# Scores of an attention's first batch in half rows of the TensorE array

## The chip, the cores and the metric

One Trainium2 chip (trn2), of which the kernel uses one core. The metric is the device time of one execution, in microseconds (us); the median of three runs of the kernel before is 1106.93 us (1106.71 to 1107.18).

## What is computed

An attention over blocks of 64 positions, whose result is fed to a two-layer network with a leaky ReLU. All inputs are float32.

```python
B, H, S, D = 8, 8, 576, 64                      # q, k, v
scores = matmul(q, k.transpose) / sqrt(D)
scores = where(pos_i // 64 >= pos_j // 64, scores, -1e9)
attn = softmax(scores)                          # sum + 1e-9 below the line
x = (attn @ v) as (B * S, H * D)                # 4608 x 512
out = maximum(0.01 * h, h) @ w_out,  h = x @ w_in   # 512 x 2048, 2048 x 512
```

## The kernel before

The work is attention for 64 heads (8 batches of 8) and a network (here FFN) over 18 chunks of 256 tokens. FFN chunks run as soon as the eight heads of their tokens are done, between the matmuls of later heads. The FFN matmuls (lines 847 and 866) take each operand as a high and a low part in fp32r: three products of one pass each, w_in as wih and wil, w_out as woh and wol, x as xh and xl (made by split_x), g as gh and gl.

The order of the work is written by a planner, class Plan. Each piece of work has a rank (roughly the head it belongs to plus a due time), one or several engines with a cost in ns, and keys that it reads and writes; run() goes through time, gives each free engine its ready piece of lowest rank, and writes the instructions down in that order. The planner's costs decide the order and on which of VectorE (DVE), ScalarE (ACT) and GpSimd (POOL) a copy or a subtraction runs; nothing is decided on the chip. multiply() is its model of TensorE: 109 ns (LOAD) and a stream per matmul, RATE = 0.449 ns per column, doubled before 8 us (SLOW).

A head's scores are cut in five tiles of up to 128 queries; tile t has kw[t] = 64, 192, 320, 448, 576 keys. The first batch (heads 0 to 7) is done in two halves so that the FFN can begin early: eight pieces "lo" with tiles 0, 1 and 2, then eight pieces "hi" with tiles 3 and 4. For these 16 pieces plain_s holds: the scores are float32 matmuls straight from qk_in (line 488), without high and low parts. q and k lie twice in qk_in, in partitions 0 to 63 and again in 64 to 127, since the host repeats them; the matmul runs over all 128 rows, so it adds each product twice, and the copy at line 464 scales q by scale / 2. Each float32 matmul is two matmul records on TensorE. Line 489 is that matmul, and line 491 its cost for the planner, four times the rate:

```python
go = lambda ...: nc.tensor.matmul(
    ap, qkt()[:rows, 0, cols], qkt()[:rows, 1, k0:k1], start=first, stop=last
)
yield 4 * RATE * (k1 - k0), go
```

The scores go to PSUM, p_s of two banks (odd "lo" pieces use p_h). order_a tells where a tile lies: in "lo" tiles 2 and 1 share bank 0 and tile 0 has bank 1; in "hi" tile 3 lies in bank 0, and tile 4, made after it, is two matmuls of 288 columns, one in each bank. After a group of scores, DVE masks (line 513) and takes the maximum (520), ACT takes the exponent (529), DVE sums and inverts (544, 545), one of three engines scales (558 to 560), TensorE transposes (594), ACT or DVE copies (ptf), and TensorE multiplies with v (664, in the shape 128 rows by 64 columns) into x.

In the same first part of the kernel the weights are brought in as 32 pieces of float64 words that DVE, ACT and POOL turn into float32 and into high and low parts (weight_piece: val, wih, wil, woh, wol). Later batches make their scores at line 498 in fp32r.

Of the kernel before, what the change touches and what calls it, by code (L numbers as in the profile page):

```python
# [57 lines left out]


LOAD = 109  # L60
RATE = 0.449
SLOW = 8000


class Plan:
# [37 lines left out]
    def run(self):  # L103
# [7 lines left out]
        since = [0] * total  # L111
        waiting = []
        ready = {e: [] for e in ("PE", "DVE", "ACT", "POOL", "SP")}
        free = dict.fromkeys(ready, 0)
        port = {"DVE": 0, "POOL": 0}
        order, now, moved, done = [], 0, 0, 0
        start, stream = 0, 0

        def offer(i):
            for k, choice in enumerate(self.ops[i][0]):  # L120
# [11 lines left out]
                if not left[j]:  # L132
                    offer(j)

        def multiply(matmuls, at):
            nonlocal start, stream
            for cost, fn in matmuls:
                if now < SLOW:
                    cost *= 2
                start = max(start + stream, max(start, at) + LOAD, now)  # L140
                stream = cost
                order.append(fn)
            return start + stream
# [4 lines left out]
        while done < total:  # L148
# [6 lines left out]
            for e, q in ready.items():  # L155
# [5 lines left out]
                if other:  # L161
                    open_ = port[other] <= now
                    can = [x for x in q if not ends[x[1]] and (open_ or (e == "DVE" and self.ops[x[1]][0][x[2]][0] == "DVE"))]
                    if not can:
                        wake.append(port[other])
                        continue
                    x = min(can)
                    q.remove(x)
                    heapq.heapify(q)
                elif e == "PE":  # L170
                    x = heapq.heappop(q)
                    if self.ops[x[1]][4] == "long":
                        self.fill = None
                    free[e] = multiply(self.ops[x[1]][0][x[2]][1], since[x[1]])
                    end(x[1], e, free[e])
                    continue
                else:
                    x = heapq.heappop(q)
# [48 lines left out]
def attention_ffn(ctx: ExitStack, tc: tile.TileContext, qk: bass.AP, v: bass.AP, w_in: bass.AP, w_out: bass.AP, out: bass.AP):  # L227
# [191 lines left out]
    def attention(i):  # L419
# [17 lines left out]
        def row(t, n, c, w):  # L437
            at, c0 = {0: (3, 256), 1: (3, 0), 2: (4, 0)}[t] if odd else (t, 0)
            return prow[y][at][:n, c0 + c : c0 + c + w]

        def pkeys(t):
            if odd:
                return [("p", 0, {0: 5, 1: 3, 2: 4}[t])]
            return [("p", y if t else 0, t)] + ([("p", 0, 5)] if kind == "hi" and t == 3 else [])
# [16 lines left out]
        rp = r0 - RP  # L461
        q_in, k_in = lambda: qkt()[:rows, 0, qa:qe], lambda: qkt()[:rows, 1, :ke]
        if plain_s:
            add(copying(qe - qa, q_in, q_in, by=scale / 2), rp, [], [qkey])
            qkd = [qkey]
        else:
            qd, khd, kld = qs[z][:, qa:qe], kh[z][:, :ke], kl[z][:, :ke]
# [14 lines left out]
        def scores(tiles):  # L482
            banks = [bank for bank, _ in tiles]
            for y, (b, (t, ap, k0, k1, c)) in enumerate(tiles):
                first, last = b not in banks[:y], b not in banks[y + 1 :]
                cols = slice(q0[t], q0[t] + P)
                if plain_s:
                    go = lambda ap=ap, cols=cols, k0=k0, k1=k1, first=first, last=last: nc.tensor.matmul(  # L488
                        ap, qkt()[:rows, 0, cols], qkt()[:rows, 1, k0:k1], start=first, stop=last
                    )  # L490
                    yield 4 * RATE * (k1 - k0), go
                    continue
                if c == BOTH:
                    moving = ks[z][:, :, k0:k1]
# [9 lines left out]

        def softmax(tiles, mms, masks, r, both=None):
            banks = sorted({(sk, bk) for _, _, bk in tiles for bk in bk})
            add([("PE", list(scores(mms)))], r, qkd, banks)
            if both is not None:
                add([merging(*both, BLK)], r, [], banks)

# [52 lines left out]
        lay = order_a[kind]  # L563
        tiles = [(t, scored(k)[:, c : c + kw[t]], (k,)) for t, k, c in lay]
        at = {t: (bk[0], ap) for t, ap, bk in tiles}
        if plain_s:
            mms = [(bk[0], (t, ap, 0, kw[t], 0)) for t, ap, bk in tiles]
        else:
            mms = [(at[t][0], (t, at[t][1], 0, kw[t], c)) for t, c in turns[kind]]
        pair = lambda ap, step: ap.rearrange("p (a b) -> p a b", b=BLK)[:, 0 : step + 1 : step]  # L570
        masks = [ap[0:64, kw[t] - 64 : kw[t]] for t, ap, _ in tiles if t]
        if kind == "full":
            masks = [pair(p_s[:BLK].rearrange("p a b -> p (a b)")[:, 384:832], 6)]
        softmax(tiles, mms, masks, r0)
        if kind != "lo":
            tiles = [(4, p_s[:, :, 0:288], (0, 1))]
# [205 lines left out]
    def bank():  # L782
# [2 lines left out]

    order_a = {
        "full": ((3, 0, 0), (2, 1, 0)),
        "lo": ((2, 0, 0), (1, 0, 320), (0, 1, 0)),
        "hi": ((3, 0, 0),),
    }  # L790
    turns = {
# [164 lines left out]
```

## Time and profile before

| what | us |
|---|---|
| median of three runs (lowest, highest) | 1106.93 (1106.71, 1107.18) |
| span of the profiled execution, first to last instruction | 1104.7 |
| what the median has beyond that span | 2.2 |
| TensorE busy (share of the span) | 1075.9 (97%) |
| VectorE, ScalarE, GpSimd busy | 808.9, 685.0, 437.8 |
| matmul records | 6792 |

The profiled execution has no time of its own beside its span, so the median less the span stands for what lies around it. A matmul record begins where its stream begins and ends some time after the next has begun, so the price of one is taken from start to start and not from its duration. A write of a PSUM tile by line 488 is called a group here: the three matmuls of a "lo" piece, or those of tile 3 or of tile 4 of a "hi" piece; there are 24. FFN start is the first matmul of line 847.

### The profile page before, as it was taken

Reading aid. Unit: us, or ns where it says so; the run is one execution under the profiler, and the core shown is the slowest. Engines: PE = TensorE matmul, PEld = TensorE weight load, DVE = VectorE, ACT = ScalarE, POOL = GpSimd, SP = SyncE. Lnnn points to the kernel's source line nnn. Section 1 sums busy time; section 2 is a strip of 40 time slices with the busy share of each in tenths; the row PEclk is TensorE's granted clock in tenths of the full one; section 3 lists DMA queues with packets and bytes.
Section 4 is the critical chain, followed back from the end, with each engine's and each line's share of the span. In section 5 each row is a group of like instructions: output and inputs, shape, how many; then the busy total and the mean of one; then the engine's idle time right before and its main releaser. Section 6 shows DMA issues by size and latency. Waiting matters only on the chain.

```text
span 1104.7 us, 19959 instructions
## 1 busy us (share of the span) xinstructions
PE 1075.9 (97%) x6792; PEld 951.1 (86%) x6792; DVE 808.9 (73%) x2001; ACT 685.0 (62%) x1664; POOL 437.8 (40%) x371
## 2 busy tenths in 40 slices
PE   5799999999999999999999999999999999999998
PEld 4577887788888999988999999989999999999997
DVE  5999867689989998976666799898989998400000
ACT  6887776577866777654655667767676766322222
POOL 2332421035754455433523455545454444412221
PEclk9999999999999999999999999999999999999999
DMA  6766432157775766654464476667676655100000
GB/s 223 219 210 203 151 115 60 52 163 210 214 205 171 204 182 199 181 168 128 129 171 120 120 216 179 202 173 208 188 209 187 203 168 161 44 20 20 1 20 20
DMA packets 94245, 166.19 MB, mean 150 GB/s; under 512 B 9664, under 2 KB 79296, under 8 KB 94144
## 3 DMA queue, kind: packets, MB, share of 16 engines
q1 hardware_dynamic: 94144, 164.93, 50.9%
q8 instruction: 53, 0.87, 0.3%
q14 instruction: 48, 0.39, 0.1%
HBM read 111.41 MB, written 53.48 MB: 149 GB/s over the span
## 4 chain that ended last, share of the span: by engine, by line
PE 77%; DVE 11%; ACT 6%; DMA 2%; issue 2%; SPq 0%; POOL 0%; ACTq 0%; DVEq 0%; POOLq 0%
PE p_h L847 29%; PE p_o L866 29%; PE p_s L498 6%; PE p_t L682 5%; PE p_t L664 4%; ACT prow L529 2%; DVE turn L745 2%; PE p_t L594 2%; DMA ptm<-way 2%; DVE nmrec L520 2%; PE p_s L488 2%; DVE qs L471 1%; ACT prow L560 1%; DVE pt L253 1%; ACT pt L243 1%
## 5 line engine op out<-in xcount | busy, mean ns | idle before, releaser
L847 PE MATMUL p_h<-xh,wih 128*128 128x256 f32 x1152 | 323.5, 281 | 1.7 <-ACT g L854 1.7
L847 PE MATMUL p_h<-xl,wih 128*128 128x256 f32 x1152 | 320.6, 278 | 0.7 <-DVE xl L253 0.6
L847 PE MATMUL p_h<-xh,wil 128*128 128x256 f32 x1152 | 319.9, 278 | 0.0
L254 POOL TENSOR_TENSOR gl<-g,gh 128x512 fp32r<-128x512 f32 x105 | 141.9, 1351 | 423.5 <-ACT gh L243 383.0
L847 PEld LDWEIGHTS p_h<-xh,wih 128*128 128x128 f32 x1152 | 216.5, 188 | 11.3 <-ACT g L854 2.1
L847 PEld LDWEIGHTS p_h<-xl,wih 128*128 128x128 f32 x1152 | 216.9, 188 | 10.6 <-DVE xl L253 1.3
L847 PEld LDWEIGHTS p_h<-xh,wil 128*128 128x128 f32 x1152 | 216.7, 188 | 0.0
L854 ACT ACTIVATE g<-p_h 128x512 f32<-128x512 f32 x144 | 85.8, 596 | 194.9 <-PE p_h L847 186.8
L529 ACT ACTIVATE prow<-p_s,nmrec 128x576 f32<-128x576 f32 (+4 forms) x308 | 160.0, 527 | 59.6 <-DVE nmrec L520 55.2
L866 PE MATMUL p_o<-woh,gh 128*128 128x512 f32 x576 | 181.2, 396 | 0.0
L866 PE MATMUL p_o<-woh,gl 128*128 128x512 f32 x576 | 179.3, 393 | 0.0
L866 PE MATMUL p_o<-wol,gh 128*128 128x512 f32 x576 | 179.0, 392 | 0.0
L254 POOL TENSOR_TENSOR pt<-ptm,pt 128x448 fp32r<-128x448 f32 x111 | 143.1, 1299 | 21.9 <-ACT pt L243 12.6
L745 DVE STREAM_TRANSPOSE turn<-prow 128x384 f32<-128x384 f32 (+3 forms) x384 | 141.2, 397 | 7.6 <-ACT prow L560 5.7
L520 DVE TENSOR_REDUCE nmrec<-p_s 128x1 f32<-128x576 f32 (+4 forms) x308 | 137.8, 480 | 2.6
L560 ACT ACTIVATE prow<-prow,nmrec 128x320 f32<-128x320 f32 (+4 forms) x231 | 110.9, 519 | 44.4 <-DVE nmrec L545 44.1
L866 PEld LDWEIGHTS p_o<-woh,gl 128*128 128x128 f32 x576 | 108.2, 188 | 24.1
L866 PEld LDWEIGHTS p_o<-wol,gh 128*128 128x128 f32 x576 | 108.2, 188 | 23.4
L498 PE MATMUL p_s<-ks,qs 128*128 128x288 f32 (+4 forms) x616 | 107.6, 307 | 3.9 <-ACT prow L529 3.6
L498 PEld LDWEIGHTS p_s<-ks,qs 128*128 128x128 f32 x616 | 89.2, 188 | 11.7 <-ACT prow L529 7.0
L866 PEld LDWEIGHTS p_o<-woh,gh 128*128 128x128 f32 x576 | 92.5, 188 | 5.9 <-issue 3.2
L243 ACT CAST pt<-ptm 128x448 fp32r<-128x448 f32 x182 | 90.7, 567 | 3.6 <-DMA ptm<-way 3.5
(83 smaller groups left out, 1422.5 us busy)
## 6 DMA issues: line engine op xcount, KB each, us to landing
way<-turn SPq DMA_DIRECT2D x192, 224.0 KB, 2.4
ptm<-way SPq DMA_DIRECT2D x192, 224.0 KB, 4.3
qk_in<-in_qk SPq DMA_DIRECT2D x56, 576.0 KB, 4.8
out<-ob SPq DMA_DIRECT2D x35, 256.0 KB, 2.4
raw<-in_w_in SPq DMA_DIRECT2D x16, 512.0 KB, 4.3
raw<-in_w_out SPq DMA_DIRECT2D x16, 512.0 KB, 4.3
v_stage<-in_v SPq DMA_DIRECT2D x48, 160.0 KB, 2.3
qk_in<-in_qk SPq DMA_DIRECT2D x8, 320.0 KB, 4.5
```

Of the source, the lines that this page charges most:

```text
L243: one = lambda: nc.scalar.copy(dst(), src())
L254: ("POOL", pool2(n), lambda: nc.gpsimd.tensor_sub(dst(), one(), two())),
L498: go = lambda ap=ap, cols=cols, moving=moving, first=first, last=last: nc.tensor.matmul(ap, qs[z][:, cols], moving, start=first, stop=last)
L520: [("DVE", dve(kw[t]), lambda t=t, ap=ap, flat=flat: nc.vector.tensor_reduce(nm[z][: qn[t], at_col[t] : at_col[t] + 1], ap[: qn[t]], axis= ...
L529: nc.scalar.activation(o, ap[: qn[t]], AF.Exp, bias=nm[z][: qn[t], at_col[t] : at_col[t] + 1], scale=1.0, accum_out=sums[z][: qn[t], at_co ...
L560: ("ACT", act(kw[t], True), lambda: nc.scalar.mul(p(), p(), by)),
L664: nc.tensor.matmul(to, vf[z][:, j], src, start=start, stop=stop)
L682: nc.tensor.matmul(to, vs[:, j, :], src, start=start, stop=stop)
L745: nc.vector.transpose(dst, src.rearrange("p (s b i) -> p s b i", b=4, i=32))
L847: nc.tensor.matmul(hh[:, i, :], w[:, d, f * P : (f + 1) * P], x[:, d, :], start=k == 0, stop=k == len(terms) - 1)
L854: add([("ACT", act(512), lambda: nc.scalar.activation(g, hh, AF.Prelu, alpha=0.01))], rank, [("h", z)], ["g"])
L866: nc.tensor.matmul(p_o[m], a[:, i, m * P : (m + 1) * P], w[:, 2 * u + i, :], start=u == 0 and k == 0, stop=u == NU - 1 and k == 5,)
```

## The change

The scores of the first batch use half of the array's rows for each matmul. Bank 0 of the two gets its scores from partitions 0 to 63 of qk_in, bank 1 from 64 to 127, so that a product is added once and q is scaled by scale. In "lo" tile 1 goes to bank 1 with tile 0 (320 columns in one bank, 256 in the other); in "hi" tile 3 is cut like tile 4, in two matmuls of 224 columns. The planner is told that such a matmul costs half of before, and that TensorE pays 100 ns (CHANGE) each time it goes from whole rows to half rows or back. Line numbers of the changed kernel are higher by 5 (scores) to 10 (transposes 604, values 674, FFN 857 and 876).

```diff
+CHANGE = 100
...
-        def multiply(matmuls, at):
-            nonlocal start, stream
+        def multiply(matmuls, at, half):
+            nonlocal start, stream, halved
+            if half != halved:
+                start, stream, halved = max(start + stream + CHANGE, now), 0, half
...
-            add(copying(qe - qa, q_in, q_in, by=scale / 2), rp, [], [qkey])
+            add(copying(qe - qa, q_in, q_in, by=scale), rp, [], [qkey])
...
-                    go = lambda ap=ap, cols=cols, k0=k0, k1=k1, first=first, last=last: nc.tensor.matmul(
-                        ap, qkt()[:rows, 0, cols], qkt()[:rows, 1, k0:k1], start=first, stop=last
+                    half = slice(64 * b, 64 * b + 64)
+                    go = lambda ap=ap, half=half, cols=cols, k0=k0, k1=k1, first=first, last=last: nc.tensor.matmul(
+                        ap, qkt()[half, 0, cols], qkt()[half, 1, k0:k1], start=first, stop=last
                     )
-                    yield 4 * RATE * (k1 - k0), go
+                    yield 2 * RATE * (k1 - k0), go
...
-            add([("PE", list(scores(mms)))], r, qkd, banks)
+            add([("PE", list(scores(mms)))], r, qkd, banks, kind="half" if plain_s else None)
...
-        if plain_s:
+        if kind == "hi":
+            tiles = [(3, p_s[:, :, 0:224], (0, 1))]
+            mms = [(k, (3, p_s[:, k, 0:224], 224 * k, 224 * k + 224, 0)) for k in range(2)]
+        elif plain_s:
...
-        "lo": ((2, 0, 0), (1, 0, 320), (0, 1, 0)),
+        "lo": ((2, 0, 0), (1, 1, 0), (0, 1, 192)),
```

The planner writes another order with these costs. On TensorE it differs from before up to row 870 of its list and is the same, row for row, behind it; DVE, ACT and POOL too differ only in the first quarter of their lists. Three places are shown (names as in the code; a number at a row's end counts equal rows in a row).

TensorE around the FFN start, before: L488 is a group of scores, L594 a transpose, L847 the FFN's first layer.

```order
107 L488 MATMUL p_s<-qk_in_124 128x448
108 L594 MATMUL p_t_99<-ident,prow_3_74 128x128
109 L594 MATMUL p_t_99<-ident,prow_4_75 128x128
110 L594 MATMUL p_t_99<-ident,prow_3_74 128x128
111 L594 MATMUL p_t_99<-ident,prow_4_75 128x128
112 L594 MATMUL p_t_98<-ident,prow_3_74 128x128
113 L594 MATMUL p_t_98<-ident,prow_4_75 128x128
114 L594 MATMUL p_t_98<-ident,prow_3_74 128x128
115 L594 MATMUL p_t_98<-ident,prow_4_75 128x128 x2
116 L488 MATMUL p_s<-qk_in_124 128x288 x2
117 L847 MATMUL p_h_100<-xh,wih 128x256
```

The same place of the changed kernel (L493 scores, L674 values, L857 FFN, L604 transposes).

```order
105 L674 MATMUL p_t_98<-ptf,vf_123 64x64
106 L493 MATMUL p_s<-qk_in_84 128x288 x2
107 L493 MATMUL p_s<-qk_in_124 128x224 x2
108 L857 MATMUL p_h_100<-xh,wih 128x256
109 L857 MATMUL p_h_100<-xl,wih 128x256
...
119 L857 MATMUL p_h_100<-xh,wil 128x256
120 L604 MATMUL p_t_99<-ident,prow_3_74 128x128
121 L604 MATMUL p_t_99<-ident,prow_4_75 128x128
```

The nine transposes of the first "hi" piece and the scores of the second one's tile 4 stood ahead of the FFN start, and now stand behind it; all that is ahead of it otherwise is the same work.

DVE of the changed kernel just ahead of that FFN start; before, the subtraction that makes xl was row 33 of POOL's list.

```order
106 L402 SCALAR_TENSOR_TENSOR val_119<-raw_116,val_119 128x512
107 L518 MEMSET p_s 64x64
108 L525 TENSOR_REDUCE nmrec<-p_s 128x1
109 L250 TENSOR_SCALAR val_120<-raw_117 128x512
110 L256 TENSOR_TENSOR xl<-xr_96,xh 128x1024
```

The subtraction moved from POOL to DVE, and the conversion to xh ahead of it from DVE to ACT.

## Rows read from the trace of the kernel before

**Rows 1.** The page's part 1, and the chain that ended last by engine (part 4).

```profile
PE 1075.9 (97%) x6792; PEld 951.1 (86%) x6792; DVE 808.9 (73%) x2001; ACT 685.0 (62%) x1664; POOL 437.8 (40%) x371
...
PE 77%; DVE 11%; ACT 6%; DMA 2%; issue 2%; SPq 0%; POOL 0%; ACTq 0%; DVEq 0%; POOLq 0%
```

**Rows 2.** Windows: length, busy us and records by engine, granted clock, DMA share, GB/s.

```profile
4.70:20.20 15.50, 12.06 (x52) 8.92 (x52) 10.13 (x33) 10.45 (x29) 3.94 (x5) 1.00 0.75 241
20.20:23.60 3.40, 0.03 (x1) 0.02 (x1) 3.27 (x11) 3.35 (x15) 0.59 (x1) 1.00 0.93 327
23.60:30.40 6.80, 6.75 (x23) 4.69 (x23) 5.05 (x15) 3.45 (x12) 0.67 (x1) 0.50 0.45 140
30.40:56.50 26.10, 19.43 (x108) 13.30 (x107) 23.56 (x66) 23.77 (x70) 9.88 (x8) 1.00 0.76 235
56.50:130.00 73.50, 73.04 (x445) 59.49 (x443) 68.77 (x149) 55.67 (x114) 21.55 (x15) 1.00 0.62 191
130.00:211.00 81.00, 81.00 (x506) 65.28 (x505) 54.84 (x145) 55.53 (x150) 16.79 (x19) 1.00 0.27 84
211.00:240.00 29.00, 29.00 (x173) 22.66 (x172) 21.59 (x62) 17.93 (x49) 4.34 (x4) 1.00 0.37 116
```

**Rows 3.** Timeline of all engines around the FFN start: start, length, instruction.

```profile
53.67 2.54 POOL L254 TENSOR_TENSOR xl<-xr,xh 128x1024 fp32r<-128x1024 f32 x1
56.50 0.50 PE L847 MATMUL p_h<-xh,wih 128*128 128x256 f32 x1
56.68 0.68 DVE L399 SCALAR_TENSOR_TENSOR val<-raw,val 128x512 int32<-128x512 int32 x1
```

**Rows 4.** TensorE's timeline, groups of scores and what follows them.

```profile
4.75 2.39 PE L488 MATMUL p_s<-qk_in 128*128 128x320 f32 x6 [4.75 <-ACT qk_in L246]
16.75 1.20 PE L488 MATMUL p_s<-qk_in 128*128 128x320 f32 x6
17.78 0.28 PE L594 MATMUL p_t<-ident,prow 128*128 128x128 f32 x1
25.49 2.23 PE L488 MATMUL p_s<-qk_in 128*128 128x320 f32 x6
27.66 2.18 PE L664 MATMUL p_t<-ptf,vf 128*64 128x64 f32 x8
113.23 1.15 PE L594 MATMUL p_t<-ident,prow 128*128 128x128 f32 x9
114.13 0.71 PE L866 MATMUL p_o<-woh,gh 128*128 128x512 f32 x2
```

**Rows 5.** TensorE's timeline inside one tile 4 group, windows that begin at each record.

```profile
123.19 0.40 PE L488 MATMUL p_s<-qk_in 128*128 128x288 f32 x1
123.43 0.65 PE L488 MATMUL p_s<-qk_in 128*128 128x288 f32 x2
123.67 0.65 PE L488 MATMUL p_s<-qk_in 128*128 128x288 f32 x2
```

**Rows 6.** TensorE's timeline at a step from whole shape to 128 by 64.

```profile
118.34 0.62 PE L866 MATMUL p_o<-woh,gh 128*128 128x512 f32 x2
118.80 0.62 PE L866 MATMUL p_o<-wol,gh 128*128 128x512 f32 x2
119.26 0.63 PE L866 MATMUL p_o<-woh,gl 128*128 128x512 f32 x2
119.81 0.43 PE L664 MATMUL p_t<-ptf,vf 128*64 128x256 f32 x1
```

**Rows 7.** DVE's groups by form, 0 to 130 us: count, busy us, mean ns, idle before.

```profile
L399 DVE SCALAR_TENSOR_TENSOR val<-raw,val 128x512 int32<-128x512 int32 x32 | 23.1, 723 | 0.1
L253 DVE TENSOR_TENSOR wol<-val,woh 128x512 fp32r<-128x512 f32 x12 | 9.3, 774 | 0.0
L244 DVE COPY ptf<-p_t 128x512 f32<-128x512 f32 x7 | 4.8, 682 | 1.1 <-PE p_t L594 1.0
```

**Rows 8.** Whom DVE waited for, 8 to 56 us: total, times, longest.

```profile
DVE p_h L513 <- PE p_h L488: 1.8, 2, 1.2
```

More of the change, by code (lines that the diff above doesn't have):

```diff
@@ L116, in run @@
         order, now, moved, done = [], 0, 0, 0
-        start, stream = 0, 0
+        start, stream, halved = 0, 0, False
         def offer(i):
@@ L173, in run @@
                         self.fill = None
-                    free[e] = multiply(self.ops[x[1]][0][x[2]][1], since[x[1]])
+                    free[e] = multiply(self.ops[x[1]][0][x[2]][1], since[x[1]], self.ops[x[1]][4] == "half")
                     end(x[1], e, free[e])
@@ L570, in attention @@
         pair = lambda ap, step: ap.rearrange("p (a b) -> p a b", b=BLK)[:, 0 : step + 1 : step]
-        masks = [ap[0:64, kw[t] - 64 : kw[t]] for t, ap, _ in tiles if t]
+        masks = [ap[0:64, kw[t] - 64 : kw[t]] for t, ap, _ in tiles if t and kind == "lo"]
         if kind == "full":
             masks = [pair(p_s[:BLK].rearrange("p a b -> p (a b)")[:, 384:832], 6)]
+        elif kind == "hi":
+            masks = [p_s[0:64, 1, 160:224]]
         softmax(tiles, mms, masks, r0)
```

## The prediction

> **What bounds the kernel now.** I read the page first: TensorE is busy for 1075.9 of 1104.7 us, and 77% of the chain that ended last is TensorE [rows 1]. So it matters where TensorE is *not* busy, and that is what the windows show [rows 2]. From the FFN start at 56.50 us [rows 3] to 240 us TensorE has 73.04 + 81.00 + 29.00 us of work in 183.5 us: a microsecond of TensorE work saved or added there moves all that follows, by as much. Ahead of 56.50 us TensorE is idle for 18.2 us (56.5 less 12.06 + 0.03 + 6.75 + 19.43), and what ends that stretch is something else: the first FFN matmul begins at 56.50, 0.29 us after POOL has ended xl (53.67 + 2.54 = 56.21) [rows 3], while VectorE is busy for 23.56 and ScalarE for 23.77 of the 26.10 us before [rows 2]. The order behind TensorE's row 870 is unchanged, which is at about 211 us in the trace, inside the full stretch. So the sum has two terms: when the FFN starts, and how much TensorE work lies behind that start. What comes later is moved along as it is.
>
> **What a group of scores costs.** A float32 matmul is two records. Inside a tile 4 group the records start at 123.19, 123.43 and 123.67 [rows 5]: 0.24 us for 288 columns, so four records take 0.97 us. By columns, tile 3 (two records of 448) takes 2 x 0.375 = 0.75 us. The three matmuls of a "lo" piece take 17.78 - 16.75 = 1.03 us, and about twice that where the engine ran at the lower of its two clocks: 27.66 - 25.49 = 2.17 us, in a stretch with a granted clock of 0.50 (1.2 GHz) [rows 2, 4].
>
> What the changed group costs no row shows, since no two matmuls of before sit in different halves of the rows. It lies between two ends. If nothing overlaps, tile 4 still has four records of 0.24 us, and tile 3 four of 0.19. If the halves run fully side by side, it is half. I take three quarters, by the order in which the records stand: bank 0's two records come first and both need rows 0 to 63, so the second waits for the first, as at 123.19 and 123.43; only then comes bank 1's first record, which can run beside it; bank 1's second is alone. That is three streams in place of four: 0.73 us for tile 4 and 0.56 for tile 3. A "lo" group goes from 576 to 416 columns, by 28%. The Trainium skill (TensorE: Matmul & The Clock Gate, Part 3: Packing small matmuls) has matmuls start and end strictly in program order and overlap when they sit in different row groups, which would give the three quarters too; no run here has shown it yet.
>
> **What a change of shape costs.** Six FFN records start 0.46 us apart in pairs (118.34, 118.80, 119.26), and the values matmul behind them, of 128 rows by 64 columns, only 0.55 us after 119.26 [rows 6]: a step from one shape to the other costs 0.09 us. The Trainium skill (TensorEngine Tiling (Array Packing), Key Properties) says that a change of tiling mode drains the engine; the trace agrees with that, at 0.09 us. I take the same for a step to half rows and back. Counting the steps in the two lists of TensorE gives 70 before and 107 now: 32 and 40 ahead of the FFN start, 34 and 63 between it and row 870. That is the part of the change that works against it.
>
> **Behind the FFN start.** Before, six tile 3 groups and six tile 4 groups lie there: 6 x 0.75 + 6 x 0.97 = 10.3 us. Now it is six and seven: 6 x 0.56 + 7 x 0.73 = 8.5 us, so -1.8. The steps add 29 x 0.09 = +2.6. The nine transposes that moved behind the start took 114.13 - 113.23 = 0.9 us [rows 4]: +0.9. Together **+1.7 us**.
>
> **Ahead of it.** xl now is VectorE's row 110. Before, VectorE had done 111 rows by 56.68 + 0.68 = 57.36 us [rows 3]. The two lists up to there hold mostly the same; the change has two wol and one wil subtraction fewer (0.77 each), one val step of line 399 or 404 fewer (0.72), one conversion to xh and half a dozen small ones fewer (about 2.2 together), two ptf copies more (0.68 each), one weight conversion more (0.4), and xl itself (about twice a wol less its fixed part, 1.3) [rows 7]. That is some 2.2 us less, so xl ends near 55.1 and the FFN starts near 55.4: -1.1 us. Then VectorE waits less for scores in the "lo" part: it stood until 7.2 us for the first group (4.75 + 2.39) [rows 4], and 1.8 us for those in p_h [rows 8]. Three of these groups took about twice the usual time (those at 4.75 and 25.49 [rows 4] and the first in p_h), where 28% of some 1.9 us of stream is 0.5 us each: -1.5. The eight new steps there fall mostly into waits, I count none. Together **-2.6 us**. ScalarE, which has four ptf copies fewer up to this point, covers the xh conversion it got; if it does not, 0.9 us of this are lost.
>
> **The sum** is -2.6 + 1.7 = -0.9 us, a span of 1103.8, and with the 2.2 us around it 1106.0 us. A measurement here can tell about 0.2%, 2.2 us, from no change; so the forecast is no change that can be told.
>
> Neither term is exact. The second holds if VectorE keeps up: it is busy for 68.77 of 73.5 us after the start [rows 2], mostly with weights. Another unknown is the clock. TensorE was idle for 3.4 us up to 23.60, and the granted clock then was 0.50 until 30.40 with 6.75 us of work in it [rows 2]. If the wait is shorter now and the clock holds, 1 to 2 us more are won (VectorE has 1.75 us free in that window); if a second such stretch appears, as much is lost. That gives my case 1103.3 to 1108.5 us.
>
> **The rivals.**
> - *Both halves fully side by side.* Each of the four records would have to run with the one of the other bank, though both of bank 0 stand ahead. Behind the start that is 6 x 0.375 + 7 x 0.48 = 5.6 us in place of 10.3, with steps and transposes -1.2; ahead, 44% of the three slow "lo" groups, -2.5, and VectorE's -1.1. In all -4.8: **1102.1 us**. No row of before has two matmuls in different halves, so none speaks against it; that all starts in [rows 5] follow the order of the records is what makes me take it second. The Trainium skill's table (TensorEngine Tiling (Array Packing), Theoretical Speedup) gives up to 2x for a dimension of at most 64; no run here shows it.
> - *No overlap at all; the change does not do what it says.* If a record of one half waits until the other is through, the streams are as long as before: behind the start 6 x 0.75 + 7 x 0.97 - 10.3 = +1.0, with steps and transposes +4.5; ahead, VectorE's -1.1 and some steps on the waits, -0.8. In all +3.7: **1110.6 us**, slower. Between this and my forecast the sum changes sign where a fifth of a group overlaps, and it is slower by 2.2 us where less than a twelfth does. For it speaks that in every row matmul starts stand one stream apart; all of those are in the same rows of the array, though.
> - *The weights set the pace.* The FFN starts earlier, but its weights come from VectorE, which has 4.7 us free in 73.5 and gets xl. Then the first chunk ends when it did, the 2.6 us are given back as waits of line 857, and +1.7 stays: **1108.6 us**. Against it: in the trace TensorE waits for no weight there.
>
> **How the numbers follow.** Three quarters 0.45 (of that 0.30 faster, 0.62 the same, 0.08 slower by the range above), side by side 0.27 (0.8 faster, 0.2 the same), no overlap 0.16 (0.75 slower, 0.25 the same), weights 0.12 (0.6 the same, 0.4 slower). Faster by over 0.2%: 0.135 + 0.216 = 0.35. Same: 0.279 + 0.054 + 0.040 + 0.072 = 0.45. Slower: 0.036 + 0.120 + 0.048 = 0.20. The range reaches from just under the second case to the third, 1101.8 to 1110.5 us; what lies outside is a second gain on top of full overlap, or a lost clock on top of none.
>
> **What would show it.** In the profile of the changed kernel the third record of a tile 4 group should start with the second, within 0.05 us, and the fourth one stream (0.24 us) later; starts in pairs from the first on mean full overlap, four even starts none. The record after a half-row group in another shape should start some 0.09 us late. The FFN should start between 53 and 55 us, and TensorE have no wait of note from there to 240 us. The prediction is wrong in its reasons if the FFN starts at 56 us or later, if line 857 waits for wih, wil or xl, or if the time behind the FFN start differs from before by more than 1 us from the +1.7.

## The result, and the profile after

The changed kernel takes **1113.44 us** (median of four runs, 1112.54 to 1115.26) beside 1107.06 (1106.71 to 1107.27) before: ratio **1.0058, interval 1.0044 to 1.0072**, slower by 0.6%. The forecast was 1106.0 us in a range of 1101.8 to 1110.5.

The page after, parts 1 and 4 (chain by engine); it answers to [rows 1].

```profile
PE 1079.5 (97%) x6808; PEld 950.4 (86%) x6808; DVE 810.2 (73%) x2007; ACT 685.0 (62%) x1661; POOL 435.6 (39%) x368
...
PE 76%; DVE 14%; ACT 5%; issue 3%; DMA 1%; POOL 0%; SPq 0%; ACTq 0%; DVEq 0%; POOLq 0%
```

The span is 1110.9 us, 6.2 more than before. Matching FFN records (the matmuls of line 857, 847 before, counted from 0 in both traces) places the loss:

| stretch | before, us | after, us | difference |
|---|---|---|---|
| up to the FFN start | 56.50 | 57.32 | +0.82 |
| FFN record 0 to 24 | 6.18 | 9.07 | +2.89 |
| FFN record 24 to 360 | 156.14 | 158.90 | +2.76 |
| the rest | 885.85 | 885.56 | -0.29 |

**The groups.** First what the change is about: one tile 4 group after. Windows of its records alone (columns as in [rows 2]: TensorE's matmuls, weight loads, clock), then the timeline of what stands behind it.

```profile
84.50:84.52 0.02, 0.01 (x2) 0.01 (x2) 1.00 1.01 307
84.52:84.84 0.32, 0.32 (x2) 0.29 (x4) 1.00 0.79 278
84.84:84.87 0.03, 0.03 (x4) 0.00 (x0) 1.00 0.77 273
```

```profile
84.51 0.76 PE L493 MATMUL p_s<-qk_in 64*128 64x288 f32 x4
85.19 0.74 PE L876 MATMUL p_o<-woh,gh 128*128 128x512 f32 x2
```

Two records run from the first 0.02 us on, no third for 0.32 us, and then the other two start together (the trace has 84.509, 84.515, 84.855 and 84.862). The halves run **fully side by side**: 85.19 - 84.51 = 0.68 us, where four streams one behind the other would take 0.97 us and the step back to whole rows besides. Of the 0.68 us 0.35 is the first pair, 0.24 the second and 0.09 the step.

**The FFN start.** All engines just ahead of it, after; it answers to [rows 3].

```profile
55.68 1.50 DVE L250 TENSOR_SCALAR val<-raw 128x512 f32<-128x512 f32 x1
56.74 0.65 PE L493 MATMUL p_s<-qk_in 64*128 64x224 f32 x4 [1.98 <-ACT prow L534]
57.10 1.21 DVE L256 TENSOR_TENSOR xl<-xr,xh 128x1024 fp32r<-128x1024 f32 x1
57.32 0.38 PE L857 MATMUL p_h<-xh,wih 128*128 128x256 f32 x1
58.37 0.19 PEld L857 LDWEIGHTS p_h<-xl,wih 128*128 128x128 f32 x1 [0.86 <-DVE xl L256]
```

The first FFN record needs only xh. It stands behind a group of scores that waited 1.98 us for ScalarE's exponent (prow). The second record starts 1.05 us later, right after xl (57.10 + 1.21 = 58.31), which VectorE makes now. The chain of work that ended last, up to the FFN start, before and then after:

```profile
53.74 1.11 PE p_t L594 x8
54.86 0.73 ACT prow L529 x2
55.64 1.24 PE p_s L488 x4
56.88 2.74 PE p_h L847 x24
```

```profile
47.41 1.22 PE p_t L674 x8
...
51.49 2.02 PE p_t L674 x8
53.51 1.29 PE p_s L493 x4
...
57.18 1.13 DVE xl L256
58.31 0.08 DVE nmrec L549
58.39 1.72 PE p_h L857 x7
```

Before, the chain has only TensorE and ScalarE from 46.06 us to the start; xl was ready 0.29 us ahead of the start and held nothing up. After, it runs through VectorE and xl. VectorE came to xl late. Whom it waited for from 8 to 58 us, the waits for transposes and for p_s, before (the one for p_h is in [rows 8]) and then after:

```profile
DVE p_s L513 <- PE p_s L488: 1.6, 1, 1.6
DVE ptf L244 <- PE p_t L594: 1.0, 2, 0.7
```

```profile
DVE ptf L247 <- PE p_t L604: 4.9, 4, 2.9
DVE p_s L518 <- PE p_s L493: 3.0, 2, 2.2
```

With the shorter ones it is 5.5 us in all before and 10.1 us after. The longest wait for scores, 2.2 us, is the one for the group at 53.51. VectorE's work is not what grew: up to the end of xl after it is busy for 40.78 us and idle for 17.53; before, up to 57.36 us, where it had done 111 rows, it was busy for 42.87 and idle for 14.49. The stretch ahead of the FFN start in windows of 4 us, before (first row) and after (the other two; columns as in [rows 2]):

```profile
52.00:56.00 4.00, 2.58 (x13) 1.60 (x14) 3.64 (x10) 3.91 (x9) 3.92 (x2) 1.00 0.71 206
```

```profile
52.00:56.00 4.00, 2.77 (x10) 1.41 (x8) 1.72 (x5) 2.79 (x5) 1.65 (x2) 0.61 0.33 92
56.00:60.00 4.00, 2.59 (x13) 2.12 (x14) 3.93 (x9) 2.04 (x4) 0.90 (x1) 0.82 0.70 232
```

VectorE was busy for 3.64 of these 4 us and now is for 1.72, ScalarE and GpSimd too are idler; and the granted clock falls to 0.61. In the trace it is at the lower of its two levels (1.2 GHz) up to 31.2 us, from 34.6 to 38.1, from 51.7 to 55.1 and from 58.5 to 61.9 us. FFN records in the last of these start 0.21 us apart in place of 0.11: the 24 records of the second row of the table take 5.02 us (0.66 of it the wait for xl) in place of 2.95. Most of the rest of that row is transposes: nine take 1.49 us where before four took 0.41.

**Behind it.** TensorE waits twice from FFN record 24 to 360 after, the longer time for xl, from GpSimd (the other wait is 0.7 us, for prow); before there was one, of 0.5 us.

```profile
PE p_h L857 <- POOL xl L257: 1.1, 1, 1.1
```

From start to start the scores there take 7.59 us in place of 8.20, for one group more; they saved more than that, since the FFN record behind a whole-row group starts 0.03 us after the group's last record and takes that record's stream into its own time. Values take 34.59 in place of 33.29 us and FFN records of line 857 42.50 in place of 41.30; the two waits are 0.65 and 1.09 us of that.

So the matmuls did what the change wants, and the time went elsewhere. Two theories are to be told apart: either the half rows themselves cost something (through the clock or the steps), or the new order does.

### The profile page after: what moved, and what is told of

Read it like the earlier page. It is cut to its first block, busy times and chain, and to the rows that moved or that the text cites. A ratio compares the mean times of both kernels' runs of the same rounds, so it can differ in the third digit from the quotient of the medians.

```text
span 1110.9 us, 19975 instructions
## 1 busy us (share of the span) xinstructions
PE 1079.5 (97%) x6808; PEld 950.4 (86%) x6808; DVE 810.2 (73%) x2007; ACT 685.0 (62%) x1661; POOL 435.6 (39%) x368
## 4 chain that ended last, share of the span: by engine, by line
PE 76%; DVE 14%; ACT 5%; issue 3%; DMA 1%; POOL 0%; SPq 0%; ACTq 0%; DVEq 0%; POOLq 0%
PE p_h L857 29%; PE p_o L876 28%; PE p_s L503 6%; PE p_t L692 5%; PE p_t L674 4%; DVE turn L755 3%; DVE nmrec L525 3%; PE p_t L604 2%; ACT prow L534 2%; DVE qs L475 1%; DVE pt L256 1%; PE p_s L493 1%; DMA way<-turn 1%; ACT prow L565 1%; ACT pt L246 1%
## 5 line engine op out<-in xcount | busy, mean ns | idle before, releaser
L857 PE MATMUL p_h<-xh,wih 128*128 128x256 f32 x1152 | 323.7, 281 | 1.7 <-ACT g L864 1.7
L857 PE MATMUL p_h<-xl,wih 128*128 128x256 f32 x1152 | 321.5, 279 | 2.4 <-POOL xl L257 1.1
L857 PE MATMUL p_h<-xh,wil 128*128 128x256 f32 x1152 | 320.6, 278 | 0.0
L257 POOL TENSOR_TENSOR gl<-g,gh 128x512 fp32r<-128x512 f32 x103 | 138.3, 1342 | 453.7 <-ACT gh L246 377.2
L857 PEld LDWEIGHTS p_h<-xh,wih 128*128 128x128 f32 x1152 | 216.9, 188 | 13.6 <-issue 2.9
L857 PEld LDWEIGHTS p_h<-xl,wih 128*128 128x128 f32 x1152 | 217.4, 189 | 12.9 <-DVE xl L256 2.4
L857 PEld LDWEIGHTS p_h<-xh,wil 128*128 128x128 f32 x1152 | 217.4, 189 | 0.0
L534 ACT ACTIVATE prow<-p_s,nmrec 128x576 f32<-128x576 f32 (+4 forms) x308 | 159.9, 526 | 61.9 <-DVE nmrec L525 55.4
```

Source lines behind the costliest of these rows:

```text
L257: ("POOL", pool2(n), lambda: nc.gpsimd.tensor_sub(dst(), one(), two())),
L534: nc.scalar.activation(o, ap[: qn[t]], AF.Exp, bias=nm[z][: qn[t], at_col[t] : at_col[t] + 1], scale=1.0, accum_out=sums[z][: qn[t], at_co ...
L857: nc.tensor.matmul(hh[:, i, :], w[:, d, f * P : (f + 1) * P], x[:, d, :], start=k == 0, stop=k == len(terms) - 1)
```

## The experiments

Ratios are to runs of the kernel before on the same chip. "Old order" is a kernel whose rows stand on every engine as before, "new order" as in the changed kernel.

### Rows and order apart

Half rows in the old order: the planner is told the old costs.

```diff
-                    yield 2 * RATE * (k1 - k0), go
+                    yield 4 * RATE * (k1 - k0), go
-            add(..., qkd, banks, kind="half" if plain_s else None)
+            add(..., qkd, banks, kind=None)
```

> Half rows on the chip, but the planner's costs of before, so that every engine's order is that of before. Clock theory (half-row matmuls leave TensorE at the lower of its two clocks for longer in the first 60 us, and that is what costs): the full clock comes clearly later than the 13.4 us of before, the first FFN matmul starts 1 to 3 us later than 56.5, and the time is 1108 to 1111 us. Order theory (the new order costs, not the half rows): the clock rises as before, FFN start at 56 us or earlier, 1104 to 1106 us, since each group behind the start is 0.1 to 0.2 us shorter. Step theory (the steps to half rows and back cost more than the overlap gives): FFN start as before, and 1 to 3 us more between it and 211 us.

Whole rows in the new order: the planner is told what the change tells it, and each matmul runs over all rows again (q scaled by scale / 2), in the layout of the changed kernel.

```diff
-                    half = slice(64 * b, 64 * b + 64)
+                    half = slice(0, rows)
```

> The changed kernel's order on every engine, row for row, but each score matmul over all 128 rows with q scaled by scale / 2. Clock theory: the full clock is back near 13 to 17 us and the first FFN matmul starts at 54 to 56 us; behind it 3 to 4 us more streams than in the changed kernel; 1107 to 1110 us. Order theory: the clock makes no difference, the time stays at 1112 us or goes above it by the longer streams, 1113 to 1117 us.

The layout alone: old order, whole rows, and of the change only what is cut and where it lies.

```diff
+            tiles = [(3, p_s[:, :, 0:224], (0, 1))]
...
-        "lo": ((2, 0, 0), (1, 0, 320), (0, 1, 0)),
+        "lo": ((2, 0, 0), (1, 1, 0), (0, 1, 192)),
```

> Whole rows for all pieces, every engine in the order of before; only the layout of the changed kernel (tile 1 in bank 1, tile 3 in two matmuls of 224 columns, one in each bank). Theory (the layout is worth nothing; of the loss in the old order all is due to the half rows): ratio 0.999 to 1.001, FFN start at 55.5 to 57.5 us, no stretch at the lower level from 35 us on. Rival (the layout itself holds VectorE or the clock back, since tile 3 ends later and in two banks): FFN start at 58 us or later, ratio 1.003 or more.

| ratio | whole rows | half rows |
|---|---|---|
| old order | 1.0000 (0.9989 to 1.0011) | 1.0067 (1.0045 to 1.0089) |
| new order | 1.0094 (1.0073 to 1.0114) | 1.0058 (1.0044 to 1.0072) |

The layout is worth nothing. **Each of the two parts costs alone, and they don't add**: in the new order half rows are no loss but by these ratios some 0.36% of gain. The stretch from FFN record 24 to 360 shows the gain in both orders: 155.88 us with the layout alone and 155.05 with half rows (old order), 160.42 and 158.90 (new order). What half rows lose in the old order lies ahead: the FFN start is at 56.43 us with the layout alone and at 62.57 with half rows, where the clock theory had 1 to 3 us; the clock there is first full at 32.1 us and at the lower level again from 45.8 to 66.3. In the new order whole rows take 1114.85 us, as the order theory said (1113 to 1117), with the FFN start at 58.53, later than with half rows (57.32).

### Is a profile's clock chance?

Both kernels once more, as they are.

> The kernel before once more, as a control on single profiles. Theory (half rows ahead of the FFN start keep TensorE at its lower clock level, so the level follows from what the kernel does): the granted clock is first full at 12 to 15 us, as in the profile before (13.4), the first FFN matmul starts at 56.2 to 56.8 us, and from FFN record 24 to 360 it takes 155.9 to 156.4 us. Rival (when the level rises and falls differs by chance from one execution to the next, so what single profiles show of it says nothing of the kernels): first full anywhere from 12 to 37 us, and an FFN start more than 1 us away from 56.5.

> The changed kernel once more, as a control on single profiles. Theory (the level follows from what the kernel does): first full at 29 us or later, as in its first profile (31.2), FFN start at 57.0 to 57.8 us, FFN record 24 to 360 in 158.4 to 159.4 us. Rival (chance): first full before 25 us in this profile, or an FFN start more than 1 us away from 57.3.

Before: the clock is first full (2.4 GHz) at 17.0 us in place of 13.4, the FFN start is at 56.60, and record 24 to 360 takes 156.14. After: 31.4, 57.42, 158.89, and the later stretches at the lower level within 0.2 us of the first profile. The theory holds for all but the first rise of before, which missed its bounds by 2 us. So these differences between the two kernels are not chance, as far as two profiles of each tell. For kernels whose runs scatter (half rows in the old order 1107.7 to 1114.6 us, in lo alone and with the dummy products, below) one profile is one of several courses.

### Which half rows cost in the old order

Four kernels in the old order. In the first three only the condition on the piece i differs (0 to 7 are lo, 8 to 15 hi; the scores of 8 and 9 lie ahead of the FFN start); the scale goes with it.

```diff
-                    half = slice(64 * b, 64 * b + 64)
+                    half = slice(64 * b, 64 * b + 64) if i >= 10 else slice(0, rows)
```

> The order of before; half rows only for the hi pieces of heads 2 to 7, whose groups stand behind the FFN start; lo and the first two hi pieces over all rows. Clock theory: up to 56 us all is as before, FFN start at 56 to 57 us; behind it the 12 groups give the 1.1 us that they gave in the first run of half rows in the old order, 0.1% under before (0.0 to 0.2%). Step theory (the steps cost more than the overlap gives): slower by 0.1 to 0.3%. If half rows lower the clock even among FFN matmuls: slower by 0.3% or more.

Measured 0.9993 (0.9981 to 1.0006), FFN start 57.29, record 24 to 360 in 155.01 us: no loss. Ahead of the start this kernel does what before does, and yet the FFN starts 0.8 us later. So much, the size of the +0.82 in the table, a start can move from one execution to another.

The lo pieces alone:

```diff
+                    half = slice(64 * b, 64 * b + 64) if i < 8 else slice(0, rows)
```

> The order of before; half rows only for the lo pieces, hi over all rows. Clock theory: nearly all of the loss of half rows in the old order is here: full clock after 20 us, FFN start at 60 to 63 us, 0.5 to 0.9% over before. Rival (the loss comes from the hi groups or is spread): less than 0.3% over before.

Measured 1.0036 (1.0015 to 1.0058), between the theory's 0.5% and the rival's 0.3%; FFN start 58.81. Its runs lie from 1105.5 (mean clock 0.997) to 1117.1 us (0.986).

The hi pieces alone:

```diff
+                    half = slice(64 * b, 64 * b + 64) if i >= 8 else slice(0, rows)
```

> Every engine in the order of before; half rows for the eight hi pieces alone (also the two hi pieces ahead of the FFN start), whole rows for lo. Theory (the half rows of lo keep the clock low, those of hi only save stream): first full at 12 to 20 us, FFN start at 55.5 to 57.5 us, FFN record 24 to 360 shorter by 1.0 to 1.3 us, time 1104.0 to 1106.0 us beside a before of 1106. Rival (half rows anywhere ahead of the FFN start bring the level down around it): a stretch at the lower level between 40 and 65 us, FFN start at 59 us or later, time 1108 us or more.

Measured 1.0023 (1.0010 to 1.0037), FFN start 59.96, as the rival said. The six hi pieces behind the start cost nothing (the first of the four kernels), so the two ahead of it are enough. TensorE's timeline there, before and with half rows for hi:

```profile
48.63 1.24 PE L488 MATMUL p_s<-qk_in 128*128 128x288 f32 x4 [0.38 <-ACT prow L529]
49.79 1.20 PE L664 MATMUL p_t<-ptf,vf 128*64 128x64 f32 x8
...
55.64 1.24 PE L488 MATMUL p_s<-qk_in 128*128 128x288 f32 x4 [0.81 <-ACT prow L529]
```

```profile
48.93 1.33 PE L493 MATMUL p_s<-qk_in 64*128 64x288 f32 x4 [0.20 <-ACT prow L534]
50.19 2.18 PE L674 MATMUL p_t<-ptf,vf 128*64 128x64 f32 x8
...
58.70 1.33 PE L493 MATMUL p_s<-qk_in 64*128 64x288 f32 x4 [1.48 <-ACT prow L534]
```

The same rows in the same order, 0.3 us apart at first. Then the values behind the scores take 2.18 in place of 1.20 us and a group of half rows 1.33, no less than whole rows took. Windows of that stretch, before and with half rows for hi (columns as in [rows 2]):

```profile
40.00:50.00 10.00, 7.10 (x41) 4.43 (x40) 9.42 (x28) 9.17 (x31) 1.94 (x2) 1.00 0.71 228
50.00:60.00 10.00, 7.57 (x49) 5.81 (x47) 9.59 (x24) 7.83 (x17) 4.13 (x2) 1.00 0.68 198
```

```profile
40.00:50.00 10.00, 7.35 (x36) 4.27 (x35) 8.70 (x26) 8.95 (x30) 1.95 (x2) 0.78 0.74 223
50.00:60.00 10.00, 6.29 (x28) 3.72 (x26) 9.14 (x17) 6.51 (x14) 3.64 (x2) 0.67 0.50 145
```

The clock, 1.00 before, is 0.78 and 0.67. In the trace it is at 1.2 GHz from 45.6 to 52.4 us, behind the first group of half rows (tile 3 at 42.79), and from 55.8 to 62.7, behind the third (53.74).

In the lo part the eight values records show the level: before they take 2.18 us at 27.66 [rows 4], and 1.20 at 14.29 and 19.02. With half rows for lo:

```profile
17.51 1.43 PE L493 MATMUL p_s<-qk_in 64*128 64x320 f32 x6
18.87 0.47 PE L604 MATMUL p_t<-ident,prow 128*128 128x128 f32 x1
...
20.64 2.18 PE L674 MATMUL p_t<-ptf,vf 128*64 128x64 f32 x8
```

These and those at 13.86 and 29.14 are at 1.2 GHz, and so is all up to 37.1 us by the trace; a group takes 18.87 - 17.51 = 1.36 us, a third more than the 1.03 of whole rows at full speed [rows 4].

Is it the rows, or that TensorE is busy for less? Half rows for all pieces, each group of scores made twice:

```diff
+                def twice():
+                    gos[-1]()
+                    for go in gos:
+                        last = go()
+                    return last
```

> Every engine in the order of before; half rows for all 16 pieces, but every group of scores is made twice in a row (the second overwrites the first), so that TensorE is busy with a group about as long as before. Theory (it is half rows as such that keep the clock low): first full at 25 us or later, FFN start at 59 us or later, time 1110 us or more. Rival (it is the shorter busy time of the groups, and the idle time that follows, that keeps it low): first full at 12 to 17 us, FFN start at 55.5 to 58 us, FFN record 24 to 360 within 0.7 us of before's 156.1, time 1105 to 1108 us beside a before of 1106.

Measured 1.0067 (1.0047 to 1.0086), first full at 33.2 us, FFN start 61.27. The time and the start tell little, since the second copies are work of their own: record 24 to 360 takes 158.87 us, and half rows made once took 155.05. The clock tells more. In the lo part the busy time's rival falls: TensorE was as busy as before, and the clock stayed low. The kernel before in its second profile, then this one:

```profile
5.00:12.00 7.00, 5.39 (x16) 4.10 (x16) 3.55 (x15) 4.48 (x12) 2.26 (x4) 1.00 0.87 294
```

```profile
5.00:12.00 7.00, 5.46 (x27) 4.83 (x28) 3.66 (x15) 4.37 (x12) 2.15 (x4) 1.00 0.84 286
40.00:50.00 10.00, 7.76 (x54) 5.51 (x54) 9.14 (x27) 8.57 (x28) 2.08 (x3) 1.00 0.88 267
```

(The column of the clock reads 1.00 ahead of the first recorded change whatever the level; the records' durations tell it.) Around the hi groups it is the other way round: made twice, they stand in a stretch at full speed from 33.2 us on (the last row), where the same groups made once stand at the lower level from 45.6 or 45.8 us (the kernel with hi alone and the one with all). So for the hi groups the shorter busy time isn't ruled out, and this one profile speaks for it.

### Bringing the clock up

Whole-row products of the identity matrix ahead of each lo group (their result is not used), in the new order with half rows, and (5 for the first two groups, 3 for the others) in the old one:

```diff
+                    if kind == "lo" and y == 0:
...
+                            for _ in range(6):
+                                nc.tensor.matmul(p_o[0][:, 0:P], later["ident"], later["ident"], start=True, stop=True)
+                            real()
```

> The changed kernel with six dummy matmuls over all 128 rows (the identity, into a PSUM tile not yet in use) ahead of each group of a lo piece, the order else the same. Clock theory: the full clock comes before 20 us and the first FFN matmul earlier than 57.3 us, although TensorE has 48 more matmuls to do; 1107 to 1111 us. Order or step theory: the dummies only add work, 1113 to 1118 us.

> Half rows in the order of before, with dummy matmuls over all 128 rows (the identity) ahead of each group of a lo piece: five ahead of the first two, three ahead of the others. Clock theory (half-row matmuls do not bring the full clock, whole-row ones do): the full clock comes before 14 us and not at 32, the first FFN matmul starts at 55 to 58 us and not at 62.6; 0.2% under to 0.3% over before. Rival (half rows delay the early part by something else, a wait or the steps): the dummies add 3 to 5 us of work, FFN start at 62 us or later, 0.7% or more over before.

Measured 1.0115 (1.0083 to 1.0147) and 1.0063 (1.0042 to 1.0085). The clock came up early, at 7.0 and 5.6 us, but neither got the time back. The first stays at full speed up to 58.2 us but for 34.3 to 37.7; VectorE starts xl at 57.07 us (57.10 in the changed kernel), and the FFN start is at 59.00. So **in the new order a clock at full speed did not make VectorE less late**, though the products are work of their own, and the profile is of the fastest of runs from 1111.7 to 1122.1 us. In the second the clock fell again from 12.5 to 19.3, from 26.1 to 29.5 and from 46.6 to 67.1 us, the last over the hi groups of half rows, and the start is at 62.46. The expectation that the clock alone is the cause fell in the new order; in the old one no run held the clock up to the start with each group of half rows made once.

### What is wrong with the new order

It was taken apart in three ways. Half rows and the planner's new costs for hi alone give a third order:

```diff
+                    yield (2 if kind == "hi" else 4) * RATE * (k1 - k0), go
+            add(..., kind="half" if kind == "hi" else None)
```

> Half rows for the pieces hi alone; lo as before (whole rows, old banks). Clock theory: up to 40 us the clock is as before (full from 13 to 24 us), FFN start at 55 to 57 us, 1104 to 1107 us. Order theory: the order is again a new one, so any time from 1105 to 1113 us. Step theory: 1 to 3 us above before.

Measured 1.0118 (1.0100 to 1.0137): its FFN start is 2.0 us earlier (54.49), and some 9 us are lost from FFN record 168 (125 us) to 264 (180 us), the longest wait 4.9 us for line 565's prow. One place that looked bad in the new order, the values of one head ahead of the next head's scores on TensorE, changed round in the planner's finished list:

```diff
+            part = order[at : at + size]
+            del order[at : at + size], whose[at : at + size]
+            order[to:to], whose[to:to] = part, [y] * size
```

> The changed kernel with one thing moved on TensorE: the scores of lo head 4 stand ahead of the values of head 2, as they do before the change, not behind them; all other lists are those of the changed kernel. Order theory (VectorE waits in the changed kernel because TensorE does values first): its waits between 8 and 58 us fall from 10.1 to 7 to 8.5 us, FFN start 1 to 2.5 us earlier, 0.35 to 0.55% over before and not 0.58%. Clock theory alone: no change, 0.55 to 0.65% over before.

Measured 1.0074 (1.0050 to 1.0098), VectorE's waits still 10 us: not that place. TensorE's new list crossed with the old lists of all others (NEW is PE alone), whole rows:

```diff
+        for e in ("PE", "DVE", "ACT", "POOL", "SP"):
+            source = new if e in NEW else old
+            lists[e] = [x for x in source if x[0] == e]
```

> Whole rows for all pieces; TensorE in the order of the changed kernel, every other engine in the order of before. The kernel with all engines in the changed order and whole rows stood at 1.0094, its FFN start 2.0 us late and FFN record 24 to 360 in 160.4 us. Theory (TensorE's own new order costs it: scores of the next piece behind values, transposes behind the FFN start, so that VectorE gets its scores late): FFN start at 58 us or later, FFN record 24 to 360 in 159 us or more, ratio 1.006 or more. Rival (the new lists of VectorE, ScalarE and GpSimd cost it, with xl on VectorE and weights between): FFN start at 55.5 to 57.3 us, FFN record 24 to 360 in 155.5 to 157.5 us, ratio 0.998 to 1.002. In between: the two lists only cost together, where each waits for the other's rows.

Measured 1.0313 (1.0292 to 1.0333): the lists fit only each other, and the crossing tells nothing of which is at fault. The other crossing was not run. Last, orders that have nothing to do with the change: whole rows, and the planner told 3.9 or 4.1 times the rate for a score in place of 4.

```diff
-                    yield 4 * RATE * (k1 - k0), go
+                    yield 3.9 * RATE * (k1 - k0), go
```

> Whole rows for all pieces, the layout of the changed kernel, no half rows and no price of a change; the planner alone is told 3.9 times the rate for a score matmul in place of 4, which writes another order (222 rows of TensorE's list stand elsewhere). Theory (the order of before is a good one that small edits of the costs lose: a new order costs whether or not it is told of half rows): ratio 1.004 or more, FFN start or the time behind it 3 us or more above before. Rival (the loss of the changed order comes from being told of half the cost): ratio 0.998 to 1.003.

> The same with 4.1 times the rate (516 rows of TensorE's list stand elsewhere). Theory: ratio 1.004 or more. Rival: 0.998 to 1.003. If this one and 3.9 differ by more than 0.5%, orders that come from nearly the same costs scatter by about what the changed order lost.

Measured **1.0092 (1.0077 to 1.0108) and 1.0096 (1.0082 to 1.0109)**. The FFN start with 3.9 (with 4.1 it is at 65.94):

```profile
64.76 0.50 PE L857 MATMUL p_h<-xh,wih 128*128 128x256 f32 x1
```

A cost of scores that differs by 2.5% loses as much as the changed one does in whole rows (1.0094). All four orders of the planner that differ from before's ahead of the FFN start (the changed one, the third one and these two) lost 0.9 to 1.2%, or 0.6% with half rows everywhere; so being told of half rows is not needed for such a loss. They lose it in different places, though. Up to FFN record 24 the orders from 3.9 and 4.1 are 6.3 and 6.2 us behind before, the changed one with whole rows 4.5, and the third one is 0.8 ahead; up to record 360 they are 6.8, 7.2, 8.7 and 10.2 us behind. What in each order costs is not shown.

Half rows behind the FFN start alone, the planner told of just them, so that TensorE's order is before's up to well behind that start:

```diff
+                    yield (2 if i >= 10 else 4) * RATE * (k1 - k0), go
+            add(..., kind="half" if plain_s and i >= 10 else None)
```

> Half rows for the six hi pieces whose scores lie behind the FFN start, whole rows for the ten ahead of it, and the planner told of just that (half the cost for those six, 100 ns for a change). The same halves in the order of before stood at 0.9993 [0.9981, 1.0006]. Theory (a new order costs by itself): ratio 1.002 or more, slower than in the order of before, by waits behind the FFN start. Rival (a planner told the truth makes the order better): ratio 0.996 to 0.999.

Measured **0.9991 (0.9980 to 1.0001)**, 1104.59 us, FFN start 56.68, record 24 to 360 in 154.78 us (-1.4). The theory that a new order costs by itself had 1.002 or more here, and missed: an order that is new only behind the start cost nothing. This is the best version found; it can't be told from before, and not from the same halves in the old order (0.9993) either.

## Why the prediction was wrong

- **The step that failed: the term ahead of the FFN start, "-2.6 us".** I counted VectorE's work up to xl in the new list (-1.1) and took its waits as shorter by what the groups save (-1.5). The start came at +0.8, and the record behind it, which needs xl, 1.05 us later. The count of the work was right: VectorE was busy for 2.1 us less, where I had 2.2. The waits were not: it was idle for 3.0 us more up to there, and from 8 to 58 us its waits rose from 5.5 to 10.1. They come from how the lists of the engines meet, which no count of rows shows. Whole rows in the same order (FFN start 58.53, xl's end 58.87) show that this is the order's doing. I priced the new order as the old one with rows moved, and it is a different one.
- **The path under that step was wrong too.** I read the 0.29 us from xl's end to the FFN start of before as cause and effect. The chain of before runs through TensorE and ScalarE there, and from 46.06 us on neither xl nor VectorE is in it; so an earlier xl alone could not have brought that start forward. After, the first record again follows a group of scores that waited for ScalarE; xl, now on VectorE, holds up the second.
- **"The second holds if VectorE keeps up", +1.7 us behind the start.** It is +5.6 (2.89 + 2.76). Of that 2.1 are 24 FFN records at 1.2 GHz and a wait for xl, 1.1 transposes in the same stretch, and 1.3 more waits than before. The order makes more than all of it: with whole rows it has 8.60 and 160.42 us in the two rows of the table, 6.7 more than before, and half rows take 1.0 off, where my groups and steps came to +0.8 (-1.8 + 2.6). The wait of line 857 for xl, which I named as a sign of wrong reasons, is there twice (until 58.37 us, and for 1.1 us until 142.16).
- **The clock was allowed for with "1 to 2 us", and as a by-product of idle time.** That half rows themselves keep it low was in no case of mine. In the old order half rows cost 0.67% in all, and the trace puts the loss in stretches at the lower level; that the clock is the whole of it is not shown. In the changed kernel the late stretches are the order's, since whole rows in it have the same (51.9 to 55.3 and 58.7 to 62.1 us). What they cost there is an estimate from the rows above: 0.8 us for the values at 51.49 (2.02 beside 1.22 at 47.41), 0.5 for the scores at 53.51 (1.29 beside 0.76 at 84.51) and 1.4 for the 24 FFN records (5.02 less the wait of 0.66, beside 2.95).
- **"Three quarters" of a group was wrong, the rival's full overlap right.** The size lay between: 13 groups behind the start take 7.59 + 0.69 = 8.28 us, 7.1 without 13 steps of 0.09, where I had 8.5 and the rival 5.6. In every group of 288 columns there the first pair takes 0.35 and not 0.24 us, which gives part of the overlap back; some whole-row groups of before begin as late (0.48 us in place of 0.375 at 70.40 and 91.69), which my price of them left out.
- **The step's 0.09 us was right**: behind an FFN record half rows start 0.205 us after it and whole rows 0.117, and behind tile 3 the FFN starts 0.28 us after the last record, whose stream takes 0.19.
- **The rival that came nearest by time, no overlap at 1110.6, was right by no step of it.** Its signs, even starts and a FFN start a little earlier, are absent.
- Open: why the order of before meets so well, row by row, and what in half rows the clock answers to. That it is the rows and not the busy time is shown for the lo groups, by one profile; for the hi groups the same profile speaks for the busy time.

## What to carry to other kernels

Where a planner writes the order, a change of one cost is two changes: price the order by itself, by running it with the old instructions, and run orders from costs a few per cent apart to see how much a new order may lose. Before a start is taken to hang on an engine, read the chain that leads to it: what ended just ahead of it need not be what it waited for. Make the faster instruction first in the old order, and only where TensorE is the bound; ahead of that, where it waits on others, a shorter matmul saved nothing here and came with the lower clock. A count of rows ahead of a point tells the work, not the waits.

## What was not expected of the hardware

Matmuls in different halves of the rows start out of the order in which the kernel writes them. TensorE's groups by form in the first lo group after, in three short windows:

```profile
L493 PE MATMUL p_s<-qk_in 64*128 64x320 f32 x1 | 0.9, 899 | 4.8 <-ACT qk_in L249 4.8
L493 PE MATMUL p_s<-qk_in 64*128 64x192 f32 x1 | 0.7, 686 | 0.0
...
L493 PE MATMUL p_s<-qk_in 64*128 64x192 f32 x2 | 1.0, 605 | 0.0
L493 PE MATMUL p_s<-qk_in 64*128 64x320 f32 x1 | 0.9, 899 | 4.8 <-ACT qk_in L249 4.8
...
L493 PE MATMUL p_s<-qk_in 64*128 64x320 f32 x2 | 1.4, 818 | 4.8 <-ACT qk_in L249 4.8
```

From 4.8 to 4.9 us one record of 320 columns (tile 2, the first in the program) and one of 192 (tile 1, the second matmul) run; from 5.3 to 5.4 the second record of 192 has begun (5.332) and that of 320, which stands ahead of it, has not (5.539, in the last window). Here each half of the rows goes through its own matmuls in order and does not wait for the other. So the order in which the two banks' matmuls are written cost nothing, where I had made the three quarters out of it: starts in the order of the program, which the prediction leaned on, are not what this trace shows.
